# Issue times and landing delays by kind of transfer in a list scheduler's model of the DMA queue (attention, then two feed-forward layers, one core)

## The chip, the cores and the metric

The kernel runs on one core of a Trainium2 chip. The metric is the device time of one execution, in microseconds (us). The profile names the engines PE (TensorE matmul; PEld is its weight load), DVE (VectorE), ACT (ScalarE), POOL (GpSimd) and SP (SyncE, which here computes nothing and issues nearly all the DMA).

## The reference

```
attention, B=8, H=8, S=576, D=64:
  k_p, v_p = mean of k, v over groups of 8 positions       (72 keys each)
  attn_out = softmax(q k_p^T / 8) v_p
x  = attn_out as [4608, 512]
h  = x @ w_in [512, 2048];  g = max(h,0) + alpha*min(h,0);  x2 = g @ w_out [2048, 512]
logits = x2 @ w_gate [512, 8];  e(n) = argmax;  p(n) = softmax(logits)[e(n)]
out[n] = p(n) * ( max(x2[n] @ w1[e(n)], 0) @ w2[e(n)] )     w1 [8,512,1024], w2 [8,1024,512]
```

## The kernel before

All products are made of fp16 pairs: every operand is split into a high and a low half (a helper `s_hi` on ACT, DVE or POOL, then `s_lo` on DVE or POOL), and a product is three matmuls. Weights are converted on the core as well: `w_in` and `w_out` in the first 180 us, and the 16 expert matrices one after the other behind them, each loaded (`ew`, L1013), measured, split into two buffers `eo`, and stored to a scratch in DRAM (`wsc<-eo`, L1056).

The work comes in four strands that share the engines. (1) Attention, by tiles of 128 tokens (`plan_tile`, 36 of them): the load of q (`qr`, L528), its largest value `m` on DVE, the split, a DMA transpose `qT` (L543), the scores `sc` (L555, PE), eight exponentials `e` on ACT (L574), the weights `Abuf` in three pieces, a DMA transpose `AT` (L605), and the product with v, `xp` (L614, PE), which becomes `xT`. Keys and values come by batch (`plan_batch`): loads `raw` (L425), means, and a DMA transpose `KTb` (L466). (2) The first layer by blocks of 256 tokens (`plan_in`): products `hp` (L804), `r` on ACT (L818) and DVE (L822), `gT`; then `plan_out`: `yp` (L846). (3) The gate by blocks (`plan_gate`): `x2`, a DMA transpose `x2T` (L879), a store `x2d` (L882), logits `gp` (L910), a rank per expert, and two scatters to `table` from POOL (L985). (4) The expert layer by slots of 128 sorted tokens (`plan_slots`): a table read `srec` (L1244), a gather `x2g` from POOL (L1251), a DMA transpose `x2gT` (L1264), products `hp` (L1276) and `op` (L1294), a scatter of the result (L1304). Slots need the tokens of every earlier stage and all 16 converted matrices.

No order is written out by hand. Each step is handed to a class `Plan` with an engine (or a choice of engines), an estimated duration, the steps it depends on, the buffers it takes (`acq`) and gives back (`rel`), and a due time (`key`). `emit` runs a list schedule while the kernel is built: among all engines it takes the step that can start first by its model, at equal times the one with the lowest key, writes out its instructions, and moves the model's times on. The order in which each engine gets its instructions is thus fixed at build time. On the chip every engine works in that order and waits on semaphores; it doesn't pass a step that waits.

A step on SP is a DMA. The model has one clock `dma` for the queue. Before the change:

```python
            if o.eng == "SP":
                dma = max(dma, t + 1.1) + o.dur
                e["t"] = max(t + 0.5, dma - AHEAD)
                o.end = dma + 0.95
            else:
                e["t"] = o.end = t + o.dur
                o.end += o.lat + LAND.get(name, 0.0)
```

So with an idle queue a transfer that starts at t lands at t + 1.1 + `dur` + 0.95, and SP is free again 0.5 us after t. `dur` is 1.0 for `qT`, `x2T` and `x2gT`, 1.8 for `AT`, 1.2 for `KTb`; for loads it is bytes / 360e3 + 0.05, and 1.85 times that for q. A user on another engine is placed 0.2 us behind the landing. The expert loads have a fixed earliest time in the model's clock, 130 + 46 n us for n = 0 to 15. The last four slots are written out behind the plan, in branches.

Of the kernel before, what the change touches and what calls it, by code (L numbers as in the profile page):

```python
# [24 lines left out]

AHEAD = 3.0

LAND = {"ACT": 0.25, "DVE": 0.2, "POOL": 0.3}

PEN = {("DVE", "POOL"): (0.1, 0.0), ("DVE", "ACT"): (0.0, 0.0), ("ACT", "DVE", "POOL"): (0.0, 1.0, 1.0)}  # L30


class Op:
    __slots__ = ("eng", "dur", "fn", "deps", "key", "lat", "acq", "rel", "n", "users", "est", "end")

    def alts(self):
        return self.eng if isinstance(self.eng, tuple) else (self.eng,)
# [2 lines left out]
class Plan:  # L40
# [3 lines left out]
    def __init__(self, pools):  # L44
        self.ops, self.pools = [], pools

    def add(self, eng, dur, fn, deps=(), key=0.0, lat=0.0, acq=(), rel=(), order=()):
        o = Op()
        o.eng, o.dur, o.fn, o.key, o.lat, o.acq, o.rel = eng, dur, fn, key, lat, acq, rel
        o.deps = [d for d in deps if d is not None]  # L50
        order = [d for d in order if d is not None]
        o.n, o.users, o.est, o.end = len(o.deps) + len(order), [], 0.0, None
        for d in o.deps:
            d.users.append((o, True))
        for d in order:
            d.users.append((o, False))
        self.ops.append(o)
        return o

    def emit(self):  # L60
# [10 lines left out]
        dma = 0.0  # L71
        left = len(self.ops)
        log = []
        while left:
            best = None
            for name, e in engs.items():
                pick = None
                for k, i, o in e["ready"]:
                    t = max(e["t"], o.est)
                    for p, c in o.acq:  # L80
                        f = free[p]
                        t = max(t, sorted(f)[c - 1]) if len(f) >= c else None
# [28 lines left out]
            log.append((t, o))  # L111
            if o.eng == "SP":
                dma = max(dma, t + 1.1) + o.dur
                e["t"] = max(t + 0.5, dma - AHEAD)
                o.end = dma + 0.95
            else:
                e["t"] = o.end = t + o.dur
                o.end += o.lat + LAND.get(name, 0.0)
# [13 lines left out]
def attn_moe_moe_kernel(ctx: ExitStack, tc: tile.TileContext, q, k, v, w_in, w_out, alpha,  # L132
# [99 lines left out]
    SPQ = 10.0  # L232
# [32 lines left out]
    def dmat(nbytes):  # L265
        return nbytes / 360e3 + 0.05
# [51 lines left out]
    def first(key, shift):  # L318

        return key + shift if key < 70 else key  # L320
# [93 lines left out]
    def plan_batch(b, dl, users):  # L414
# [5 lines left out]
        for w in range(2):  # L420
            for c in range(nc_):
                def load(w=w, c=c):
                    sh = [SP_, hn, PL * D]
                    raws[w, c] = big(sh, F32, "raw0") if b == 0 else wk.tile(sh, F32, tag="raw", name="raw", bufs=2)
                    Y.dma_start(out=raws[w, c],  # L425
                                in_=(k, v)[w][b, hn * c:hn * c + hn].rearrange("h (s r) d -> s h (r d)", r=PL))

                def reduce(eng, w=w, c=c):
                    if c == 0:
                        kp[w] = wk.tile([SP_, H, D], F32, tag="kp", name="kp", bufs=2)  # L430
                    r, o_ = raws.pop((w, c)), kp[w][:, hn * c:hn * c + hn, :]
                    if eng == "DVE":
                        V.tensor_reduce(out=o_, in_=r.rearrange("p h (r d) -> p h d r", r=PL), axis=AX.X, op=ALU.add)
                        return
                    n = PL * D // 2
                    while n >= 2 * D:
                        G.tensor_tensor(out=r[:, :, 0:n], in0=r[:, :, 0:n], in1=r[:, :, n:2 * n], op=ALU.add)  # L437
                        n //= 2
                    G.tensor_tensor(out=o_, in0=r[:, :, 0:D], in1=r[:, :, D:2 * D], op=ALU.add)
                o = add("SP", dmat(72 * 2048 * hn), load, key=dl - 28 + (8 * w + c) * 8 / nc_, acq=[(pl, 1)])  # L440
                red.append(add(EITHER, (0.15 + hn * 0.87, pool(448 * hn) + 0.6), reduce, [o] + red[-1:],
                               key=dl - 26 + (8 * w + c) * 8 / nc_, rel=[(pl, 1)], acq=[("kp", 1)] if c == 0 else []))

# [48 lines left out]
                 rel=[("kp", 1)])  # L492
        o3 = add("DVE", 0.22, lambda: V.tensor_copy(kc[0:SP_, :, 3, :], kc[0:SP_, :, 0, :]), [o1], key=dl - 6)
        o4 = add("DVE", 0.22, lambda: V.tensor_copy(kc[0:SP_, :, 2, :], kc[0:SP_, :, 1, :]), [o2], key=dl - 5)
        oKT[b] = add("SP", 1.2, kT, [o2, o3, o4], key=dl - 4 - SPQ, acq=[("KT", 1)], rel=[("kc", 1)])
        o = osc[1]
        o1 = add(ANY, his(512), vhi, [o], key=dl - 4, acq=[("VS", 1)])
        o2 = add(EITHER, stt(512), vlo, [o1], key=dl - 4, acq=[("vlo", 1)], rel=[("kp", 1)])
        o3 = add("SP", 0.5, vdma, [o1], key=dl - 4)
# [19 lines left out]
    def plan_tile(i):  # L519
# [104 lines left out]
        def xlo():  # L624
            s_lo(xTt[j][:, 1, :, sl], xTt[j][:, 0, :, sl], c["xp"], S14)

        ends = [b for b in bs if LAST[b] == i]
        o = add("SP", dmat(262144) * 1.85, load, key=first(dl - 30, -6), acq=[("q", 1), ("att", 1)])
        o = add("DVE", dve(512), q1, [o], key=dl - 18)
        o = chain("DVE", pow2s(lambda: (c["m"], c["inv"], c["s"])), [o], dl - 18)  # L630
        o_s = o
        o = add(ANY, his(512), q2, [o], key=dl - 17, acq=[("qs2", 1)])
        o = add(EITHER, stt(512), lambda e: s_lo(c["qs"][:, :, 1, :], c["qs"][:, :, 0, :], c["q"], c["s"], e), [o], key=dl - 17,
                rel=[("q", 1)])
        o = add("SP", 1.0, q4, [o], key=dl - 16 - SPQ, acq=[("qT", 1)], rel=[("qs2", 1)])
# [10 lines left out]
        o = add(ANY, his(576), ahi, [o, o_c1], key=dl - 9, acq=[("A", 1)])  # L646
        o1 = add(EITHER, (dve(576), pool(576)), alo, [o], key=dl - 8, rel=[("e", 1)])
        o2 = add(("DVE", "ACT"), (0.22, 0.57), ahi2, [o], key=dl - 8)
        o = add("SP", 1.8, aT, [o1, o2], key=dl - 7 - SPA, acq=[("AT", 1)], rel=[("A", 1)])
        o = add("PE", pe(16, 128), av, [o] + [z for b in bs for z in oVS[b]], key=dl - 4, acq=[("gps", 1)],  # L650
                rel=[("AT", 1)] + [("VS", 1)] * len(ends))
        o = oXh[i] = add("ACT", act(512), xhi, [o, oXh.get(i - 1)], key=dl - 3, acq=[("xT", 1)] if half == 0 else [])
# [204 lines left out]
    def plan_gate(j):  # L857
# [5 lines left out]
        for t in range(2):  # L863
# [25 lines left out]
            o = add("SP", 1.0, y4, [o], key=k_ - SPY, acq=[("x2T", 1)])  # L889
            oT.append(o)  # L890
            oS.append(add("SP", dmat(262144), y5, [o], key=k_ + 1, rel=[("x2", 1)]))

        def ct_(t, p0, n, b):
            def f():
# [104 lines left out]
        oG2[j] = o  # L999
        oD = []  # L1000
        for t in range(2):
            oD.append(add("POOL", 1.1, lambda t=t: r3(t), [o, o4, o_tc] + oD, key=key + 6, lat=2.5,
                          rel=[("rec", 1)] if t else []))
        return oS, oD

# [1 line left out]
    def plan_expert(e, w, t0):  # L1007
# [50 lines left out]
        lds = [add("SP", dmat(1 << 20), lambda c=c: load(c), [oW["w_out"][-1]], key=t0 + c, acq=[("ew", 1), ("big", 1)]) for c in range(2)]  # L1058
        for x in lds:
            x.est = EXP0 + EXPD * (2 * e + w)  # L1060
        for c in range(4):
# [5 lines left out]
        for c in range(4):  # L1067
            ls = []
            for z in range(2):
                h = ph = add(ANY, his(512), lambda eng, c=c, z=z: hi(c, z, eng), [o, ph], key=t0 + 17 + 4 * c + 2 * z,  # L1070
                        acq=[("eo", 1)] if z == 0 else [])
                ls.append(add(EITHER, (1.0, 2.1), lambda eng, c=c, z=z: lo(c, z, eng), [h], key=t0 + 18 + 4 * c + 2 * z,
                              rel=[("ew", 1), ("big", 1)] if c % 2 and z else []))
            outs.append(add("SP", dmat(1 << 19), lambda c=c: store(c), ls, key=t0 + 20 + 4 * c, rel=[("eo", 1)]))
        return outs, o


# [134 lines left out]
    def plan_slots(c0, lo, n_slots, oD, o_x2, o_tab, o_exp, base, cond):  # L1212
# [3 lines left out]
        for i in range(n_slots):  # L1216
# [108 lines left out]
                continue  # L1325
            if n == cond + 1:
                tt = "big"
            o = add("SP", 0.1, tok, [o_r] + o_tab, key=key - 20, acq=[("srec", 1)])
            o = oGa[n] = add("POOL", 1.1, gather, [o] + o_x2, key=key - 18, lat=2.5, acq=[(tg, 1)])
            o_x = add("SP", 1.0, xT, [o], key=key - 15, acq=[(tt, 3 if tt == "big" else 1)], rel=[(tg, 1)])  # L1330
            oXt[n] = o_x

            if n >= cond:
# [113 lines left out]
```

## Time and profile before

| | us |
|---|---|
| median of 3 runs (lowest, highest) | 1445.33 (1442.6, 1445.35) |
| the profiled execution | 1447.14 |
| its span, first to last instruction | 1445.4 |
| PE busy | 1266.9 |
| DVE, POOL, ACT busy | 891.2, 778.7, 592.7 |

The profiled execution is 1.8 us above the median of the runs, and its span 1.7 us below its own time. A row of the timeline gives start, duration, engine, line, operation, the tile written and those read, a count, and in brackets the idle time before it and what ended that. Rows on SPq are DMA issues: their duration is the time that SP spent on the issue, not that of the transfer. The wait for a DMA is read off as the start of the user that was released by it.

### The profile page before, as it was taken

Reading aid. Unit: us, or ns where it says so; the run is one execution under the profiler, and the core shown is the slowest. Engines: PE = TensorE matmul, PEld = TensorE weight load, DVE = VectorE, ACT = ScalarE, POOL = GpSimd, SP = SyncE. Lnnn points to the kernel's source line nnn. Section 1 sums busy time; section 2 is a strip of 40 time slices with the busy share of each in tenths; the row PEclk is TensorE's granted clock in tenths of the full one; section 3 lists DMA queues with packets and bytes.
Section 4 is the critical chain, followed back from the end, with each engine's and each line's share of the span. In section 5 each row is a group of like instructions: output and inputs, shape, how many; then the busy total and the mean of one; then the engine's idle time right before and its main releaser. Section 6 shows DMA issues by size and latency. Waiting matters only on the chain. (4 is left out here: it accounts for less than half of the span.)

```text
span 1445.4 us, 30543 instructions
## 1 busy us (share of the span) xinstructions
PE 1266.9 (88%) x11555; PEld 875.0 (61%) x11555; DVE 891.2 (62%) x2051; ACT 592.7 (41%) x1324; POOL 778.7 (54%) x847
## 2 busy tenths in 40 slices
PE   0157799889898989999899999999799999999997
PEld 0145455646655755666576667765676776777674
DVE  7998788779667968868877777654252332332222
ACT  3786555536454645645564556541010110110010
POOL 6788967668677867647665666464122122112111
PEclk9998999999999999999999999999999999999999
DMA  9983397766777766676577476536658843593334
GB/s 241 290 196 91 98 222 149 191 152 163 190 149 171 201 190 130 176 195 153 126 189 199 122 149 146 172 103 197 168 133 240 198 91 74 167 304 104 74 96 166
DMA packets 314504, 237.21 MB, mean 164 GB/s; under 512 B 258351, under 2 KB 267695, under 8 KB 309488
## 3 DMA queue, kind: packets, MB, share of 16 engines
q1 hardware_dynamic: 306800, 214.98, 59.7%
q0 software_dynamic: 7552, 20.23, 4.7%
q8 instruction: 92, 1.51, 0.5%
q14 instruction: 60, 0.49, 0.1%
HBM read 263.52 MB, written 54.34 MB: 220 GB/s over the span
## 5 line engine op out<-in xcount | busy, mean ns | idle before, releaser
L804 PE MATMUL hp<-xT,w_in_hl 128*128 128x256 f16 x3456 | 409.8, 280 | 30.0 <-DVE r L822 22.4
L846 PE MATMUL yp<-w_out_hl,gT 128*128 128x512 f16 x1728 | 394.7, 386 | 9.6 <-POOL w_out_hl L201 5.4
L804 PEld LDWEIGHTS <-w_in_hl 128*128 128x128 f16 x3456 | 341.5, 100 | 83.1 <-DVE r L822 31.0
L846 PEld LDWEIGHTS <-gT 128*128 128x128 f16 x1728 | 168.2, 99 | 211.6 <-issue 22.6
L1276 PE MATMUL hp<-x2gT,ws 128*128 128x128 f16 x3744 | 217.9, 222 | 12.7 <-DMA x2gT<-x2g 8.1
L1276 PEld LDWEIGHTS <-ws 128*128 128x128 f16 x3744 | 215.7, 99 | 17.9 <-issue 12.0
L1294 PE MATMUL op<-ws,ht 128*128 128x512 f16 x936 | 205.7, 379 | 1.9 <-issue 1.9
L1282 ACT ACTIVATE hr<-hp 128x512 f32<-128x512 f32 x78 | 46.6, 597 | 374.1 <-PE hp L1276 369.9
L1294 PEld LDWEIGHTS <-ht 128*128 128x128 f16 x936 | 90.7, 98 | 107.6 <-issue 2.4
L574 ACT ACTIVATE e<-sc,nb,esc 128x72 f32<-128x72 f32 x288 | 116.3, 417 | 92.8 <-DVE inv L276 55.0
L1251 POOL DMA_INDIRECT x2g<-x2d,srec x41 | 43.5, 1061 | 202.3 <-DMA srec<-table 147.2
L822 DVE SCALAR_TENSOR_TENSOR r<-r,al,hp 128x256 f32<-128x256 f32 x288 | 124.0, 471 | 29.4 <-ACT r L818 29.1
L437 POOL TENSOR_TENSOR raw<-raw 72x256 f32<-72x256 f32 (+3 forms) x144 | 98.8, 686 | 65.2 <-DMA raw<-in_v_dram 30.4
L201 POOL TENSOR_TENSOR gT<-r,gT 128x512 f16<-128x512 f32 x99 | 124.8, 1260 | 8.3
L1286 DVE CAST ht<-hr 128x512 f16<-128x512 f32 x78 | 33.5, 430 | 151.5 <-ACT hr L1282 150.0
L183 ACT ACTIVATE gT<-r,cg 128x512 f16<-128x512 f32 x144 | 103.6, 724 | 55.9 <-DVE r L822 32.1
L183 ACT ACTIVATE eo<-ew,es 128x512 f16<-128x512 f32 x128 | 85.9, 713 | 97.7 <-DMA wsc<-eo 49.9
L1304 POOL DMA_INDIRECT out_dram<-so,srec x39 | 39.3, 1008 | 157.4 <-DVE cb L1299 60.4
L1301 DVE TENSOR_SCALAR so<-op,cb 128x512 f32<-128x512 f32 x39 | 29.3, 751 | 145.4 <-PE op L1294 145.3
L818 ACT ACTIVATE r<-hp 128x512 f32<-128x512 f32 x144 | 86.1, 598 | 75.0 <-POOL gT L201 49.4
L200 POOL TENSOR_SCALAR r<-r,cg 128x512 f32<-128x512 f32 x99 | 76.5, 772 | 60.9 <-ACT gT L183 59.9
L201 POOL TENSOR_TENSOR eo<-ew,eo 128x512 f16<-128x512 f32 x61 | 85.0, 1394 | 5.1
(221 smaller groups left out, 1524.9 us busy)
## 6 DMA issues: line engine op xcount, KB each, us to landing
ws<-wsc SPq DMA_DIRECT2D x166, 1024.0 KB
ew<-in_moe_w_dram SPq DMA_DIRECT2D x32, 1024.0 KB
wsc<-eo SPq DMA_DIRECT2D x64, 512.0 KB
x2d<-x SPq DMA_DIRECT2D x36, 256.0 KB
qr<-in_q_dram SPq DMA_DIRECT2D x32, 256.0 KB
w_in_f<-in_moe_w_in_dram SPq DMA_DIRECT2D x16, 512.0 KB
w_out_f<-in_moe_w_out_dram SPq DMA_DIRECT2D x16, 512.0 KB
raw<-in_k_dram SPq DMA_DIRECT2D x56, 144.0 KB
```

The costliest lines, as they stand in the source:

```text
L183: A.activation(out=hi, in_=src, func=ACTF.Copy, scale=s)
L200: G.tensor_scalar(out=src, in0=src, scalar1=s, scalar2=0.0, op0=ALU.mult, op1=ALU.add)
L201: G.tensor_tensor(out=lo, in0=src, in1=hi, op=ALU.subtract)
L437: G.tensor_tensor(out=r[:, :, 0:n], in0=r[:, :, 0:n], in1=r[:, :, n:2 * n], op=ALU.add)
L574: A.activation(out=c["e"][x], in_=c["scv"][x], func=ACTF.Exp, bias=c["nb"][:, z // 4, z % 4:z % 4 + 1], scale=c["esc"], accum_out=c["sm"][x])
L804: T.matmul(out=hp, lhsT=wt[:, a, kk, (m % 4) * 128:(m % 4 + 1) * 128], rhs=xTt[j][:, x, kk, :], start=(n == 0), stop=(n == 3 * KD - 1))
L818: A.activation(out=c["r"], in_=hps[j, m // 2], func=ACTF.Relu, scale=-1.0)
L822: V.scalar_tensor_tensor(out=c["r"][:, z], in0=c["r"][:, z], scalar=al1[:, m - 1 + z:m + z], in1=hps[j, m // 2][:, z], op0=ALU.mult, op1=A ...
L846: T.matmul(out=ypt[i], lhsT=gT[j][x][:, m, o_ * 128:(o_ + 1) * 128], rhs=W["w_out"][part][:, w, m % 4, :], start=(m == 0 and x == 0 and w ...
L1276: T.matmul(out=hp[:, f, :], lhsT=ws[kk // 2][:, kk % 2, a, ff * 128:(ff + 1) * 128], rhs=c["xT"][:, x * KD + kk, :], start=(z == 0), stop= ...
L1282: A.activation(out=c["hr", f4], in_=c["hp", f4], func=ACTF.Relu, scale=S24)
L1294: T.matmul(out=op, lhsT=c["ht"][:, x, f, :], rhs=ws[f // 4][:, f % 4, w, :], start=(f == 0 and x == 0 and w == 0), stop=(f == KF2 - 1 and ...
```

## The change

The model gets two tables by kind of transfer, and each DMA step a `kind`. SP is held for the time in `ISSUE` (0.45 us where a kind has none), and a transfer lands later by the time in `LATE`. The scatters to `table` and the gathers, issued on POOL, get a longer latency in the model (`lat` 2.5 to 4.0, and 2.5 to 3.3). No step, buffer, due time or duration is changed; what can differ in the program is the order in which steps are written out and the engine chosen for steps that have a choice.

```diff
+ISSUE = {"qT": 1.4, "AT": 1.9, "yT": 1.4, "kT": 1.5, "xT": 1.4, "v": 1.6, "tok": 0.8}
+LATE = {"kv": 1.5, "q": 1.0, "ew": 2.5, "st": 1.0, "qT": 1.0, "AT": 1.2, "yT": 1.0, "kT": 0.8, "v": 2.0, "x2": 2.0, "xT": 1.0}
...
                 dma = max(dma, t + 1.1) + o.dur
-                e["t"] = max(t + 0.5, dma - AHEAD)
-                o.end = dma + 0.95
+                e["t"] = max(t + ISSUE.get(o.kind, 0.45), dma - AHEAD)
+                o.end = dma + 0.95 + LATE.get(o.kind, 0.0)
...
-        o = add("SP", dmat(262144) * 1.85, load, key=first(dl - 30, -6), acq=[("q", 1), ("att", 1)])
+        o = add("SP", dmat(262144) * 1.85, load, kind="q", key=first(dl - 30, -6), acq=[("q", 1), ("att", 1)])
...
-        o = add("SP", 1.8, aT, [o1, o2], key=dl - 7 - SPA, acq=[("AT", 1)], rel=[("A", 1)])
+        o = add("SP", 1.8, aT, [o1, o2], kind="AT", key=dl - 7 - SPA, acq=[("AT", 1)], rel=[("A", 1)])
...
-            oD.append(add("POOL", 1.1, lambda t=t: r3(t), [o, o4, o_tc] + oD, key=key + 6, lat=2.5,
+            oD.append(add("POOL", 1.1, lambda t=t: r3(t), [o, o4, o_tc] + oD, key=key + 6, lat=4.0,
                           rel=[("rec", 1)] if t else []))
...
-            o = oGa[n] = add("POOL", 1.1, gather, [o] + o_x2, key=key - 18, lat=2.5, acq=[(tg, 1)])
-            o_x = add("SP", 1.0, xT, [o], key=key - 15, acq=[(tt, 3 if tt == "big" else 1)], rel=[(tg, 1)])
+            o = oGa[n] = add("POOL", 1.1, gather, [o] + o_x2, key=key - 18, lat=3.3, acq=[(tg, 1)])
+            o_x = add("SP", 1.0, xT, [o], kind="xT", key=key - 15, acq=[(tt, 3 if tt == "big" else 1)], rel=[(tg, 1)])
```

The other kinds are given in the same way: `kv` to the loads `raw`, `kT` to `KTb`, `v` to the two moves inside `VSb` (L477, L478), `qT`, `yT` to `x2T`, `x2` to the store `x2d`, `ew` to the expert loads, `st` to the expert stores, `tok` to the table read. The loads of `w_in` and `w_out` and of the slots' weights get none.

## Rows read from the trace of the kernel before

**Rows 1.** Busy time by stretch: from:to, length, engines, granted clock, DMA share, GB/s:
```profile
0.00:82.00 82.00, 8.40 (x103) 6.68 (x104) 69.14 (x115) 50.13 (x94) 59.23 (x70) 1.00 1.02 257
82.00:180.00 98.00, 70.64 (x524) 50.04 (x523) 79.82 (x134) 62.62 (x99) 87.06 (x81) 0.91 0.44 119
180.00:600.00 420.00, 379.00 (x3066) 251.70 (x3064) 328.50 (x790) 218.51 (x536) 303.66 (x364) 0.96 0.74 177
600.00:1000.00 400.00, 388.00 (x3150) 259.07 (x3151) 282.14 (x722) 214.11 (x516) 245.07 (x254) 0.98 0.61 155
...
1060.00:1419.74 359.74, 355.67 (x4001) 259.01 (x3999) 102.11 (x200) 39.41 (x66) 69.68 (x67) 1.00 0.58 156
```

**Rows 2.** Waits of PE from 180 to 1000 us: total, times, longest:
```profile
PE xp L614 <- DMA AT<-Abuf: 16.5, 9, 3.2
PE hp L804 <- DVE r L822: 15.3, 9, 5.3
PE gp L910 <- DMA x2T<-x: 10.1, 4, 3.2
```

**Rows 3.** Timeline of PE, stalls between 180 and 1000 us:
```profile
226.25 0.36 PE L910 MATMUL gp<-wg,x2T 128*128 128x16 f16 x8 [3.24 <-DMA x2T<-x]
...
278.58 5.41 PE L804 MATMUL hp<-xT,w_in_hl 128*128 128x256 f16 x48 [0.20 <-DVE r L822]
...
305.26 0.66 PE L614 MATMUL xp<-AT,VSb 128*64 128x128 f16 x16 [2.31 <-DMA AT<-Abuf]
...
376.91 7.08 PE L804 MATMUL hp<-xT,w_in_hl 128*128 128x256 f16 x48 [3.80 <-DVE r L822]
...
535.70 8.32 PE L804 MATMUL hp<-xT,w_in_hl 128*128 128x256 f16 x48 [5.31 <-DVE r L822]
...
601.73 0.66 PE L614 MATMUL xp<-AT,VSb 128*64 128x128 f16 x16 [1.85 <-DMA AT<-Abuf]
...
765.71 0.66 PE L614 MATMUL xp<-AT,VSb 128*64 128x128 f16 x16 [0.40 <-DMA AT<-Abuf]
...
862.80 0.70 PE L614 MATMUL xp<-AT,VSb 128*64 128x64 f16 x32 [0.34 <-DMA AT<-Abuf]
```

**Rows 4.** Timeline from 370 to 390 us, DVE and ACT ahead of a stall:
```profile
372.22 0.69 DVE L178 TENSOR_REDUCE m<-qr 128x1 f32<-128x512 f32 x1 [4.58 <-DMA qr<-in_q_dram]
...
373.20 0.41 ACT L574 ACTIVATE e<-sc,nb,esc 128x72 f32<-128x72 f32 x1 [10.66 <-DVE inv L272]
```

**Rows 5.** Busy time just behind a stall, columns as in rows 1:
```profile
535.70:544.00 8.30, 8.30 (x53) 6.35 (x54) 6.39 (x11) 5.98 (x13) 7.80 (x9) 0.64 1.07 330
```

**Rows 6.** Timeline of SP's DMA issues ahead of such stalls, from four stretches:
```profile
215.31 3.88 SPq L879 DMA_TRANSPOSE x2T<-x  x1
...
299.22 3.06 SPq L605 DMA_TRANSPOSE AT<-Abuf  x1
...
368.19 1.27 SPq L528 DMA_DIRECT2D qr<-in_q_dram  x1
...
596.88 1.82 SPq L605 DMA_TRANSPOSE AT<-Abuf  x1
```

**Rows 7.** Timeline of PE, the first product of the first layer:
```profile
83.90 5.82 PE L804 MATMUL hp<-xT,w_in_hl 128*128 128x256 f16 x35 [1.69 <-DVE xT L198]
...
106.37 1.07 PE L614 MATMUL xp<-AT,VSb 128*64 128x128 f16 x16 [6.73 <-DMA AT<-Abuf]
```

**Rows 8.** The line of `AT`, duration of the issue in ns, min/median/max:
```profile
L605 SPq DMA_TRANSPOSE AT<-Abuf x36: 1611/2746/5080, 62.0 to 942.6; - x36
```

**Rows 9.** The line of `x2T`, columns as in rows 8:
```profile
L879 SPq DMA_TRANSPOSE x2T<-x x36: 1237/1367/7391, 186.6 to 1029.0; - x36
```

**Rows 10.** The line of the table scatters, issue on POOL to landing:
```profile
DMA to landing us min/median/max: 3.7/5.0/11.3
```

**Rows 11.** Timeline of DVE ahead of the first product, pieces of the conversion:
```profile
73.42 1.20 DVE L178 TENSOR_REDUCE m<-w_in_t 128x1 f32<-128x1024 f32 x1
...
75.15 2.63 DVE L198 SCALAR_TENSOR_TENSOR w_in_hl<-w_in_t,sw,w_in_hl 128x1024 f16<-128x1024 f32 x1
```

More of the change, by code (lines that the diff above doesn't have):

```diff
@@ L33 @@
 class Op:
-    __slots__ = ("eng", "dur", "fn", "deps", "key", "lat", "acq", "rel", "n", "users", "est", "end")
+    __slots__ = ("eng", "dur", "fn", "deps", "key", "lat", "acq", "rel", "n", "users", "est", "end", "kind")
     def alts(self):
@@ L45, in __init__, with add @@
         self.ops, self.pools = [], pools
-    def add(self, eng, dur, fn, deps=(), key=0.0, lat=0.0, acq=(), rel=(), order=()):
+    def add(self, eng, dur, fn, deps=(), key=0.0, lat=0.0, acq=(), rel=(), order=(), kind=None):
         o = Op()
+        o.kind = kind
         o.eng, o.dur, o.fn, o.key, o.lat, o.acq, o.rel = eng, dur, fn, key, lat, acq, rel
@@ L439, in reduce @@
                     G.tensor_tensor(out=o_, in0=r[:, :, 0:D], in1=r[:, :, D:2 * D], op=ALU.add)
-                o = add("SP", dmat(72 * 2048 * hn), load, key=dl - 28 + (8 * w + c) * 8 / nc_, acq=[(pl, 1)])
+                o = add("SP", dmat(72 * 2048 * hn), load, kind="kv", key=dl - 28 + (8 * w + c) * 8 / nc_, acq=[(pl, 1)])
                 red.append(add(EITHER, (0.15 + hn * 0.87, pool(448 * hn) + 0.6), reduce, [o] + red[-1:],
@@ L494, in plan_batch @@
         o4 = add("DVE", 0.22, lambda: V.tensor_copy(kc[0:SP_, :, 2, :], kc[0:SP_, :, 1, :]), [o2], key=dl - 5)
-        oKT[b] = add("SP", 1.2, kT, [o2, o3, o4], key=dl - 4 - SPQ, acq=[("KT", 1)], rel=[("kc", 1)])
+        oKT[b] = add("SP", 1.2, kT, [o2, o3, o4], kind="kT", key=dl - 4 - SPQ, acq=[("KT", 1)], rel=[("kc", 1)])
         o = osc[1]
@@ L498, in plan_batch @@
         o2 = add(EITHER, stt(512), vlo, [o1], key=dl - 4, acq=[("vlo", 1)], rel=[("kp", 1)])
-        o3 = add("SP", 0.5, vdma, [o1], key=dl - 4)
+        o3 = add("SP", 0.5, vdma, [o1], kind="v", key=dl - 4)
         o4 = add("SP", 0.3, lambda: Y.dma_start(out=VS[b][2 * SP_ - 128:3 * SP_ - 128, 1], in_=st["vlo"]), [o2],
@@ L634, in plan_tile @@
                 rel=[("q", 1)])
-        o = add("SP", 1.0, q4, [o], key=dl - 16 - SPQ, acq=[("qT", 1)], rel=[("qs2", 1)])
+        o = add("SP", 1.0, q4, [o], kind="qT", key=dl - 16 - SPQ, acq=[("qT", 1)], rel=[("qs2", 1)])
         o_e = add("DVE", tiny(len(bs)), esc, [o_s] + [oSK[b] for b in bs], key=dl - 13)
@@ L888, in plan_gate @@
             o = add("DVE", dve(512), y3, [o], key=k_, rel=[("y", 1)])
-            o = add("SP", 1.0, y4, [o], key=k_ - SPY, acq=[("x2T", 1)])
+            o = add("SP", 1.0, y4, [o], kind="yT", key=k_ - SPY, acq=[("x2T", 1)])
             oT.append(o)
-            oS.append(add("SP", dmat(262144), y5, [o], key=k_ + 1, rel=[("x2", 1)]))
+            oS.append(add("SP", dmat(262144), y5, [o], kind="x2", key=k_ + 1, rel=[("x2", 1)]))
         def ct_(t, p0, n, b):
@@ L1056, in store @@
             Y.dma_start(out=wsc[r:r + 128, 2048 * c:2048 * (c + 1)], in_=cv[c].rearrange("p n c f -> p (n c f)"))
-        lds = [add("SP", dmat(1 << 20), lambda c=c: load(c), [oW["w_out"][-1]], key=t0 + c, acq=[("ew", 1), ("big", 1)]) for c in range(2)]
+        lds = [add("SP", dmat(1 << 20), lambda c=c: load(c), [oW["w_out"][-1]], kind="ew", key=t0 + c, acq=[("ew", 1), ("big", 1)]) for c in range(2)]
         for x in lds:
@@ L1073, in plan_expert @@
                               rel=[("ew", 1), ("big", 1)] if c % 2 and z else []))
-            outs.append(add("SP", dmat(1 << 19), lambda c=c: store(c), ls, key=t0 + 20 + 4 * c, rel=[("eo", 1)]))
+            outs.append(add("SP", dmat(1 << 19), lambda c=c: store(c), ls, kind="st", key=t0 + 20 + 4 * c, rel=[("eo", 1)]))
         return outs, o
@@ L1327, in plan_slots @@
                 tt = "big"
-            o = add("SP", 0.1, tok, [o_r] + o_tab, key=key - 20, acq=[("srec", 1)])
-            o = oGa[n] = add("POOL", 1.1, gather, [o] + o_x2, key=key - 18, lat=2.5, acq=[(tg, 1)])
-            o_x = add("SP", 1.0, xT, [o], key=key - 15, acq=[(tt, 3 if tt == "big" else 1)], rel=[(tg, 1)])
+            o = add("SP", 0.1, tok, [o_r] + o_tab, kind="tok", key=key - 20, acq=[("srec", 1)])
+            o = oGa[n] = add("POOL", 1.1, gather, [o] + o_x2, key=key - 18, lat=3.3, acq=[(tg, 1)])
+            o_x = add("SP", 1.0, xT, [o], kind="xT", key=key - 15, acq=[(tt, 3 if tt == "big" else 1)], rel=[(tg, 1)])
             oXt[n] = o_x
```

## The prediction, made before the result was known

> **What bounds the kernel now.** I read the busy time by stretch first, to see where PE, the busiest engine, is idle. The reader is to see five stages in [rows 1]. Up to 82 us PE is busy for 8.4 us: attention of the first tiles and the conversion of `w_in` come first, and DVE is full. From 82 to 180 us PE is idle for 27.4 us. From 180 to 1000 us it is busy for 767.0 of 820 us, so 53.0 us are lost in the steady state, 41.0 of them before 600 us. Behind 1060 us it is busy for 355.7 of 359.7 us; nothing is to be had there. The end therefore moves with the time at which the expert slots can start, and that with what PE loses before 1000 us.
>
> The waits of PE come next. Of the 53.0 us, 16.5 us in 9 waits are for `AT` and 10.1 us in 4 for `x2T`, both DMA transposes, and 15.3 us in 9 waits for DVE's `r` [rows 2]. Then the timeline around single stalls [rows 3]: two of the longest waits for `r`, 3.80 us at 376.91 and 5.31 us at 535.70, begin at a DMA as well. Ahead of the first, DVE stood for 4.58 us in front of `m<-qr`, for a load of q; ACT, waiting for DVE, stood for 10.66 us in front of the exponentials, with the first layer's `r` queued behind them; and PE ran out of free `hp` buffers [rows 4]. The second I put down to the same cause by its likeness. So 16.5 + 10.1 + 9.1 = 35.7 us of PE's loss have a late transfer at their root.
>
> A stall also costs clock. The same 48 matmuls take 5.41 us with the clock up and 7.08 and 8.32 us behind those two stalls [rows 3]; the mean granted clock of the 8.3 us behind the second is 0.64, a mixture of 2.4 and 1.2 GHz [rows 5]. The smaller difference, 1.67 us, is my price for one such drop.
>
> **What the change does, part by part.** It adds and removes no instruction; the planner's order is all that moves, with the choice of engine for the halves. So its price is that of the stalls that it removes and makes.
>
> *Landings.* By the old model `AT` is in the hands of its user 1.1 + 1.8 + 0.95 + 0.2 = 4.05 us after SP takes it up, by the new one 5.25. The trace shows 305.26 - 299.22 = 6.04 and 601.73 - 596.88 = 4.85 us [rows 3, 6]: the old figure is below both, the new one between them. `x2T` goes from 3.25 to 4.25, where a stalled one shows 226.25 - 215.31 = 10.94; q from 3.69 to 4.69, where the one above shows 372.22 - 368.19 = 4.03 [rows 4, 6]. So the direction is right. A step planned later lets the engine do something else first, and a stall shrinks by at most what the model adds. For `AT` that is 7 x 1.2 + 0.40 + 0.34 = 9.1 us (two of the nine stalls are shorter than 1.2), for `x2T` 4 x 1.0 = 4.0, for q 2 x 1.0 = 2.0: 15.1 us. In the first 180 us one wait for `AT` of 6.73 us [rows 7] gives another 1.2. Sum 16.3 us as the upper end, if at each of these places PE has other work that is ready.
>
> The lower end is nothing, if what is put first was also waiting. From 600 us on PE is 97% busy and work is at hand; before that it is 90% busy [rows 1]. Between the ends I take one half, 8 us, since 41 of the 53 us lie where work is scarcer.
>
> *Clock.* At most every stall that goes takes its drop along: 15 stalls x 1.67 = 25 us. A stall of 2.3 us that becomes 1.1 us may still cost the drop, so the lower end is nothing. I take 3 drops, 5 us: the shorter stalls are the ones that vanish whole.
>
> *Issue time.* The old model frees SP after 0.5 us, the new one after 1.9 us for `AT` and 1.4 us for `x2T`; measured medians are 2.75 and 1.37 us [rows 8, 9]. SP does the same work as before, so this costs nothing by itself; it moves loads that are planned behind a transpose to where the chip had them anyway. What hides an issue that is planned too late is the buffer it fills; if that is empty, DVE stands in front of `m<-qr` once more, 4.58 us at the one place shown [rows 4]. I count neither.
>
> *Scatters and gathers.* The scatter to `table` was modelled at 1.1 + 2.5 + 0.3 = 3.9 us and becomes 5.4; measured from issue to landing are 3.7 at least and 5.0 in the median [rows 10]. The second scatter of a pair waits for the first and POOL with it, with the split `gT` behind. The gain on PE lies between nothing and the rest of its waits for `r`, 15.3 - 9.1 = 6.2 us [rows 2, 3]; I take none.
>
> *Choice of engine.* A step that moves to another engine changes that engine's load. DVE is busy for 328.5 and POOL for 303.7 of 420 us from 180 to 600 [rows 1], so both have room; counted at nothing. Without that room a moved half would delay `gT` by its own length.
>
> Sum: 8 + 5 = 13 us off. The profiled execution of 1447.1 becomes 1434; its span of 1445.4 plus the 1.7 us around it, less 13. It is 1.8 us above the median of the runs, so the median goes from 1445.3 to about **1432.5 us**. Upper end of the gain 16.3 + 25 + 6 = 47, lower end 0.
>
> **One rule weighed.** The two `AT` rows say that 3.85 us from issue to landing, the old model's figure without its 0.2, is too short: 6.04 and 4.85 us [rows 3, 6]. The Trainium skill, "DMA: Bandwidth & Descriptors", section "Anatomy of one DMA", fits a DMA (there one issued from GpSimd) by 2.0 us + bytes / 436e3. `AT` has 128 x 16 x 128 x 2 = 524,288 bytes, which gives an estimate of 3.2 us; by it the old model was late enough, the added 1.2 us would buy nothing, and the sum would be 0 rather than 13. The trace disagrees with that figure for this transfer.
>
> **The rivals.**
>
> *The start becomes longer* (slower). The first product of a full block comes at 83.90 us and waits for `xT` [rows 7], which is the end of a chain with four transfers in it: the loads of q and k, `qT` beside `KTb`, and `AT`. All get 0.8 to 1.5 us more, the loads of `w_in` nothing. So at each the planner can put a piece of the conversion in front of attention's next step, on DVE, which is busy for 69 of 82 us [rows 1], and such a piece takes 1.20 to 2.63 us [rows 11]. Four pieces cost 4.8 to 10.5 us, and nothing hides them: PE has no other work yet. If the chip's transfers land before the piece is done, that is pure loss. With the upper end and a steady gain of only 4 us: 1445.3 + 10.5 - 4 = 1452. It decides from a first block that starts more than the steady state's gain later, 13 us in my sum, so behind about 97 us; with a steady gain of 4 behind 88 us. For it: DVE is the full engine there. Against it: due times put early attention first where both are ready.
>
> *The change doesn't do what it says* (no change). The stalls come not from the landing that the model had wrong but from transfers that meet others in the queue: 10.94 us for one `x2T` whose issue alone took 3.88 us, 4.85 against 6.04 for equal `AT`s [rows 6]. A constant of 1.0 can't foresee that; old stalls go and others come: 1445, within 3 us. By the Trainium skill's fit above it would be this case too.
>
> *Everything goes right* (faster by more): the stalls with a transfer at the root vanish with half of the drops: 16.3 + 13 = 29, 1416.
>
> **How the numbers follow.** Forecast 0.50, start longer 0.26, no change 0.14, everything right 0.10. 0.2% is 2.9 us, about what a measurement of this kernel can tell from no change. Faster takes the forecast and everything right: 0.60. No change: 0.14, of which 0.02 goes to slower, since reordering without a gain can as well lose 3 us: 0.12. Slower 0.28. The forecast's own range is 1422 (twice the drops, and three quarters of the stall time) to 1441 (a quarter of the sum). The range for all, with some 0.1 left out at either end: 1416, where everything goes right, to 1454, just above the longer start.
>
> **What would show it.** Right: waits of PE for `AT` and `x2T` from 180 to 1000 us fall from 26.6 to below 18 us; PE's busy time of that stretch rises in share; fewer stretches at the half clock; first block still between 80 and 90 us; expert slots begin some 13 us earlier, and the time from there to the end is the same. Wrong: the first block later than 90 us; equal waits of PE under other names, above all for DVE's `r`; expert conversions (whose earliest times are fixed in the planner's clock, which now runs slower against the work) crowding DVE and POOL before 600 us.

## The result, and the profile after

| | before | after |
|---|---|---|
| median of the runs (lowest, highest), us | 1443.96 (1437.24, 1445.35), 4 runs | 1393.83 (1389.46, 1400.39), 4 runs |
| the profiled execution, its span, us | 1447.14, 1445.4 | 1400.39, 1398.4 |
| mean granted clock of TensorE | 0.972 | 0.984 |

The ratio is 0.9666, 95% interval 0.9616 to 0.9715: 3.3% faster. Forecast were 1432.5 us, 0.9% below the 1445.3 us known then, in a range that ended at 1416. The four executions differ by 8 us before and by 11 us after, and the profiled one after is the slowest of its four; so the spans below differ by 47.0 us where the medians differ by 50.1. The four lines added at the top of the file shift the line numbers by 4 (`hp` is L808, `yp` L850, `AT` L609, `x2T` L883).

To see where the 47.0 us of the span went, both traces are cut at equal work and not at equal times: where block 1, 2, 14 and 17 of the first layer start their first product `hp`, and where slot 4 of the expert layer does. The counts of PE's matmuls in the cuts agree within 2. Busy time by stretch, before (columns as in [rows 1]):

```profile
0.00:118.80 118.80, 35.40 (x327) 28.28 (x327) 101.82 (x171) 79.01 (x138) 91.82 (x106) 0.97 0.95 242
118.80:208.90 90.10, 72.55 (x522) 42.68 (x520) 70.56 (x138) 47.04 (x88) 72.39 (x70) 0.94 0.43 115
208.90:826.00 617.10, 564.43 (x4566) 377.27 (x4563) 474.12 (x1147) 329.54 (x807) 432.62 (x495) 0.96 0.70 168
826.00:960.60 134.60, 134.26 (x1143) 91.81 (x1140) 93.06 (x235) 77.92 (x193) 80.29 (x79) 1.00 0.60 151
960.60:1055.20 94.60, 84.02 (x790) 61.39 (x789) 40.27 (x140) 16.84 (x28) 28.83 (x30) 0.95 0.56 154
1055.20:1445.40 390.20, 376.24 (x4227) 273.57 (x4224) 111.37 (x224) 42.39 (x71) 72.72 (x70) 0.99 0.57 152
```

And after:

```profile
0.00:122.00 122.00, 35.64 (x328) 28.50 (x329) 105.46 (x176) 82.64 (x141) 103.94 (x113) 0.97 0.92 236
122.00:198.90 76.90, 69.45 (x523) 41.83 (x521) 63.59 (x129) 40.70 (x83) 65.69 (x67) 0.98 0.48 125
198.90:780.80 581.90, 548.11 (x4564) 370.77 (x4560) 477.28 (x1154) 328.30 (x801) 438.09 (x495) 0.99 0.78 179
780.80:915.70 134.90, 134.30 (x1144) 91.89 (x1141) 95.29 (x238) 78.36 (x194) 74.45 (x76) 1.00 0.60 153
915.70:1013.00 97.30, 82.44 (x790) 59.78 (x789) 48.03 (x152) 16.93 (x29) 28.18 (x29) 0.93 0.62 157
1013.00:1398.40 385.40, 374.69 (x4227) 272.00 (x4224) 109.11 (x214) 42.42 (x71) 73.60 (x69) 0.99 0.54 153
```

Line by line the lengths differ by +3.2, -13.2, -35.2, +0.3, +2.7 and -4.8 us: 10.0 us are gained up to block 2, 35.2 us from block 2 to block 14, and 1.8 us in all behind that. Of the 35.2 us, 16.3 us are busy time (564.43 to 548.11 for the same matmuls, at a mean granted clock of 0.96 and 0.99), and 18.9 us are idle time (52.7 to 33.8). The reader is to see that nearly half of the gain of that stretch is not in any wait: it is the clock. The engines' loads hardly moved (DVE 474.1 to 477.3 us, POOL 432.6 to 438.1, ACT 329.5 to 328.3), so the choice of engine, counted at nothing, took little load off any of them.

The waits of PE from 180 to 940 us after, the answer to [rows 2]:

```profile
PE hp L808 <- DVE r L826: 17.5, 9, 5.6
PE xp L618 <- DMA AT<-Abuf: 6.0, 4, 2.7
PE gp L914 <- DMA x2T<-x: 4.1, 5, 1.9
```

Waits for the two transposes fell from 26.6 to 10.1 us; those for `r` did not fall (15.3 to 17.5).

The timeline of PE after, first with the answer to [rows 7], then two stalls of the steady stretch:

```profile
89.17 13.97 PE L808 MATMUL hp<-xT,w_in_hl 128*128 128x256 f16 x107 [1.19 <-DVE xT L202]
...
310.00 2.79 PE L808 MATMUL hp<-xT,w_in_hl 128*128 128x256 f16 x24 [2.50 <-DVE r L826]
...
458.10 4.46 PE L808 MATMUL hp<-xT,w_in_hl 128*128 128x256 f16 x24 [2.80 <-DVE r L826]
```

The first full block begins 5.3 us later than before (89.17 against 83.90), as the rival of the longer start had it: DVE begins with the conversion of `w_out` 4.4 us earlier, now ahead of that product (its first piece in the timeline of DVE, before and after).

```profile
83.83 1.44 DVE L721 SCALAR_TENSOR_TENSOR w_out_t<-wc,w_out_t 128x1024 int32<-128x1024 int32 x1
```
```profile
79.42 1.90 DVE L725 SCALAR_TENSOR_TENSOR w_out_t<-wc,w_out_t 128x1024 int32<-128x1024 int32 x1
```

And yet the start as a whole got shorter. It ends with the conversion of `w_out`, on which the first `yp` waits. POOL's last piece of it, before and after (timeline of POOL):

```profile
176.35 2.50 POOL L201 TENSOR_TENSOR w_out_hl<-w_out_t,w_out_hl 128x1024 f16<-128x1024 f32 x1
```
```profile
161.69 2.55 POOL L205 TENSOR_TENSOR w_out_hl<-w_out_t,w_out_hl 128x1024 f16<-128x1024 f32 x1
```

PE's waits for these pieces between block 1 and block 2, before and after:

```profile
PE yp L846 <- POOL w_out_hl L201: 5.4, 3, 4.1
PE yp L846 <- DVE w_out_hl L198: 2.4, 1, 2.4
```
```profile
PE yp L850 <- POOL w_out_hl L205: 1.8, 2, 1.4
```

Of the 13.2 us gained there, 6.0 us are these waits, 4.1 us other idle time, above all PE's waits for `r` (5.7 to 1.0), and 3.1 us busy time at a higher clock (0.94 to 0.98).

### The profile page after: what moved, and what is told of

The parts are those of the page before. It is cut to its first block, busy times and chain, and to the rows that moved or that the text cites. A ratio compares the mean times of both kernels' runs of the same rounds, so it can differ in the third digit from the quotient of the medians.

```text
span 1398.4 us, 30543 instructions
## 1 busy us (share of the span) xinstructions
PE 1244.6 (89%) x11555; PEld 864.8 (62%) x11555; DVE 898.7 (64%) x2060; ACT 589.4 (42%) x1316; POOL 783.9 (56%) x845
## 5 line engine op out<-in xcount | busy, mean ns | idle before, releaser
L808 PE MATMUL hp<-xT,w_in_hl 128*128 128x256 f16 x3456 | 400.7, 277 | 28.9 <-DVE r L826 20.3
L850 PE MATMUL yp<-w_out_hl,gT 128*128 128x512 f16 x1728 | 385.4, 380 | 2.4 <-POOL w_out_hl L205 1.8
L808 PEld LDWEIGHTS <-w_in_hl 128*128 128x128 f16 x3456 | 337.5, 99 | 76.8 <-DVE r L826 21.7
L850 PEld LDWEIGHTS <-gT 128*128 128x128 f16 x1728 | 165.9, 98 | 201.3 <-issue 10.0
L1280 PE MATMUL hp<-x2gT,ws 128*128 128x128 f16 x3744 | 215.3, 220 | 13.2 <-DMA x2gT<-x2g 11.9
L1280 PEld LDWEIGHTS <-ws 128*128 128x128 f16 x3744 | 212.8, 98 | 18.8 <-issue 14.0
L205 POOL TENSOR_TENSOR gT<-r,gT 128x512 f16<-128x512 f32 x106 | 129.7, 1224 | 8.8
L441 POOL TENSOR_TENSOR raw<-raw 72x256 f32<-72x256 f32 (+3 forms) x138 | 105.6, 766 | 27.9 <-DMA raw<-in_v_dram 12.1
L204 POOL TENSOR_SCALAR r<-r,cg 128x512 f32<-128x512 f32 x106 | 83.2, 785 | 60.1 <-ACT gT L187 55.8
L205 POOL TENSOR_TENSOR eo<-ew,eo 128x512 f16<-128x512 f32 x63 | 79.3, 1259 | 5.3
```

What stands on the lines that cost most here:

```text
L204: G.tensor_scalar(out=src, in0=src, scalar1=s, scalar2=0.0, op0=ALU.mult, op1=ALU.add)
L205: G.tensor_tensor(out=lo, in0=src, in1=hi, op=ALU.subtract)
L808: T.matmul(out=hp, lhsT=wt[:, a, kk, (m % 4) * 128:(m % 4 + 1) * 128], rhs=xTt[j][:, x, kk, :], start=(n == 0), stop=(n == 3 * KD - 1))
L850: T.matmul(out=ypt[i], lhsT=gT[j][x][:, m, o_ * 128:(o_ + 1) * 128], rhs=W["w_out"][part][:, w, m % 4, :], start=(m == 0 and x == 0 and w ...
L1280: T.matmul(out=hp[:, f, :], lhsT=ws[kk // 2][:, kk % 2, a, ff * 128:(ff + 1) * 128], rhs=c["xT"][:, x * KD + kk, :], start=(z == 0), stop= ...
```

## The experiments

Each was compared with the kernel before on the same chip, whose medians there were 1437.3 to 1440.7 us; "ratio" is to that kernel, with its 95% interval. The edits are shown in short form, against the changed kernel where nothing else is said. Theories: **A**, the landing delays of the transposes, before which PE stood; **B**, those of loads and stores, before and behind which DVE, ACT and POOL stood; **C**, the issue times; **D**, luck, any reshuffled order being better than the one before.

### One part alone, and a reshuffle

Issue times alone (`e1_issue_only`):

```diff
-LATE = {"kv": 1.5, ...}
+LATE = {}
...
-lat=4.0 / lat=3.3
+lat=2.5 / lat=2.5
```

> Only the issue times by kind; landing delays and the POOL latencies as before. Theory A (the landing delays did it: the engines no longer stand in order behind a transfer that the model lands too early): within 10 us of before, 1434 to 1454, PE's waits for AT and x2T about as before (22 us in the steady blocks). Theory C (the issue times did it: SP's queue is planned where the chip has it): most of the gain, 1395 to 1410. Theory D (luck: the order before was a poor one and any reshuffle does better): faster by 20 us or more as well.

Measured 1441.2, ratio 1.0032 (1.0008 to 1.0056): within 0.3% of before. C alone is out, and so is D in its simple form, that any reshuffle does better.

Landing delays alone (`e2_late_only`):

```diff
-ISSUE = {"qT": 1.4, ...}
+ISSUE = {}          # and ISSUE.get(o.kind, 0.5)
...
-lat=4.0 / lat=3.3
+lat=2.5 / lat=2.5
```

> Only the landing delays by kind; SP's issue time is 0.5 us for all and the POOL latencies are as before. A: nearly the whole gain, 1390 to 1405, with few stretches at the half clock. C: within 10 us of before. D: anywhere between 1395 and 1445, without relation to PE's waits for DMA.

Measured 1423.6, ratio 0.9916 (0.9890 to 0.9942): a quarter of the gain. A had said 1390 to 1405 and C within 10 us of before; both miss. The longest of its waits of PE from block 2 to block 14 grew, against 10.1 us in 4 before:

```profile
PE gp L914 <- DMA x2T<-x: 20.0, 7, 4.9
```

POOL's latencies alone (`e3_lat_only`: `ISSUE = {}` with 0.5 for all, `LATE = {}`, `lat` 4.0 and 3.3):

> Only the latencies of the table scatters and the gathers, both issued on POOL; SP's model as before. A and C: within 10 us of before, 1434 to 1454. D: faster by 20 us or more, as any reshuffle.

Measured 1439.1, ratio 1.0019 (0.9999 to 1.0038): no gain, as A and C had it.

A reshuffle without a better model (`e6_nudge_up`, the kernel before with one constant nudged):

```diff
-                o.end = dma + 0.95
+                o.end = dma + 1.0
```

> The kernel before with one constant nudged, the landing of every SP transfer 1.0 instead of 0.95 us after the queue's clock: the order is reshuffled, and the model is no better. A and C: 1434 to 1454, the scatter of orders being below 10 us. D: the order before was an unlucky one, so this one comes out 20 us or more faster.

Measured 1441.0, ratio 1.0021 (0.9996 to 1.0045). Every engine's order is another one, some 100 steps change between DVE and POOL, about as many as in the change, and the time is the same within 0.3%. Four orders made without longer landing delays on SP (before, and these three without `LATE`) lie between 1.000 and 1.003: the gain is neither luck of reshuffling nor a matter of steps that move to another engine.

### Which landing delays, and with what

Landing delays and issue times, POOL's latencies as before (`e11_late_issue`: the change with `lat=2.5` in both places):

> Landing delays and issue times by kind, the POOL latencies as before. Alone, the landing delays gave 0.8% and the issue times nothing; together with the POOL latencies 3.3%. Theory E (landing and issue need each other: with landings right, PE still stood 25.9 us in front of x2T, whose issue comes late because SP is modelled as free after 0.5 us): most of the gain, 1385 to 1400, PE's waits for x2T below 10 us. Theory F (landing and POOL latencies need each other): about as the landing delays alone, 1415 to 1425. Theory D (luck of one order): no relation, 1390 to 1430.

Measured 1403.1, ratio 0.9748 (0.9695 to 0.9801). With the issue times, worth nothing alone, this is 1.7% faster than the landing delays without them. E still misses its range (1385 to 1400) by 3 us, and PE's waits for `x2T` fell from 20.0 to 14.0 us, not below 10. The 1.7% compare one order with one other.

Landing delays of the five transposes alone, and of loads and stores alone (`e4_late_transposes`, `e5_late_rest`; `ISSUE` and `lat` as before):

```diff
+LATE = {"qT": 1.0, "AT": 1.2, "yT": 1.0, "kT": 0.8, "xT": 1.0}                       # e4
+LATE = {"kv": 1.5, "q": 1.0, "ew": 2.5, "st": 1.0, "v": 2.0, "x2": 2.0}              # e5
```

> Of the landing delays only those of the five DMA transposes; nothing else. Theory A (it is PE in front of its transposes): as all landing delays together, 1418 to 1428. Theory B (it is DVE, ACT and POOL in front of loads and behind stores): as before, 1432 to 1445.

> Of the landing delays only those of the loads and stores (kv, q, ew, st, v, x2); nothing else. B: as all landing delays together, 1418 to 1428, with DVE's and ACT's waits for DMA down. A: as before, 1432 to 1445.

Measured 1415.1, ratio 0.9814 (0.9784 to 0.9844), and 1423.0, ratio 0.9885 (0.9852 to 0.9919). Each alone does as well as both together without issue times (0.9916) or better. Neither A nor B is out, and the parts don't add.

The waits tell the two apart where the times don't. PE's waits from 180 to 1000 us, to be held against [rows 2], with e4 first and then e5:

```profile
PE gp L914 <- DMA x2T<-x: 6.5, 4, 2.8
PE xp L618 <- DMA AT<-Abuf: 5.7, 3, 3.1
```
```profile
PE xp L618 <- DMA AT<-Abuf: 24.0, 9, 8.8
PE hp L808 <- DVE r L826: 1.4, 3, 0.9
```

And DVE's waits for the loads of q in the same stretch, before, in e4 and in e5:

```profile
DVE m L178 <- DMA qr<-in_q_dram: 42.1, 12, 6.9
```
```profile
DVE m L182 <- DMA qr<-in_q_dram: 35.3, 15, 4.3
```
```profile
DVE m L182 <- DMA qr<-in_q_dram: 18.2, 6, 4.9
```

The four orders with the old landings show what reshuffling alone does: `AT` 11.1 to 21.5 us, `x2T` 9.0 to 18.1, `r` 11.6 to 23.5, q 29.0 to 42.1. Delays of the transposes took the waits for the two transposes below that, and those for `r` to 7.8 us; delays of loads and stores took the waits for q and for `r` below it, and those for `AT` above it. So what the model lands later is waited for less in these two orders, and the fall of `r` to 1.4 us speaks for late loads at its root, as the prediction read it. It is no rule for every order: with both groups delayed (e2) PE stood before `x2T` for 20.0 us.

Landing delays and issue times of the transposes (`e13_transposes_both`; `lat` as in the change):

```diff
-ISSUE = {"qT": 1.4, "AT": 1.9, "yT": 1.4, "kT": 1.5, "xT": 1.4, "v": 1.6, "tok": 0.8}
+ISSUE = {"qT": 1.4, "AT": 1.9, "yT": 1.4, "kT": 1.5, "xT": 1.4}
-LATE = {"kv": 1.5, "q": 1.0, "ew": 2.5, ...}
+LATE = {"qT": 1.0, "AT": 1.2, "yT": 1.0, "kT": 0.8, "xT": 1.0}
```

> Landing delays and issue times for the five DMA transposes alone, POOL's latencies as in the change; loads, stores and the moves of v as before. Theory A with E (PE in front of transposes that the model issues and lands too early): nearly the whole gain, 1390 to 1405, waits of PE for x2T and AT below 12 us from block 2 to block 14. Theory B has a share of its own: 1405 to 1420, with waits of DVE for q and of POOL for the raw loads as long as before.

Measured 1413.2, ratio 0.9809 (0.9765 to 0.9854). A with E misses its range by 8 us, and B's (1405 to 1420) holds; DVE's waits for q, 33.2 us from block 2 to block 14 against 41.1, stayed long, as B had it. The issue times and POOL's latencies added nothing to e4 (0.9814). The waits of PE from block 2 to block 14 for `AT`, before, and for both transposes in e13:

```profile
PE xp L614 <- DMA AT<-Abuf: 16.1, 8, 3.2
```

```profile
PE xp L618 <- DMA AT<-Abuf: 18.4, 7, 4.4
...
PE gp L914 <- DMA x2T<-x: 1.3, 2, 0.8
```

`AT` was modelled as in the change, and PE stood before it for 18.4 us, no less than before the change (16.1). With the same figures for `AT` it was 1.6 us in e11 and 5.4 us in the change. So a transfer's own delay in the model doesn't by itself set the wait for that transfer.

The changed kernel nudged in the same way (`e8_after_nudge`, 0.95 to 1.0 in the change):

> The changed kernel with the same nudge as the kernel before got, 1.0 instead of 0.95: another order by a model that is as good. If the gain is the model's, within 10 us of the changed kernel, 1383 to 1403. If the changed kernel has a lucky order (D), it falls back by 15 us or more, to 1405 to 1435.

Measured 1393.8, ratio 0.9682 (0.9652 to 0.9712): another order, the same gain, as the model's theory had it.

### Where: the start and the rest

The new model for steps placed before 150 us of the planner's clock only, and behind it only (`e14_start_only`, with `lat=2.5`; `e15_steady_only`):

```diff
-                e["t"] = max(t + ISSUE.get(o.kind, 0.45), dma - AHEAD)
-                o.end = dma + 0.95 + LATE.get(o.kind, 0.0)
+                e["t"] = max(t + (ISSUE.get(o.kind, 0.45) if t < 150.0 else 0.5), dma - AHEAD)    # e15: t >= 150.0
+                o.end = dma + 0.95 + (LATE.get(o.kind, 0.0) if t < 150.0 else 0.0)                # e15: t >= 150.0
```

> Landing delays and issue times by kind only for steps that the model places before 150 us; behind that, and for POOL's latencies, the old model. Theory G (two separate gains: about 10 us at the start, where the conversion of w_out ends earlier, and some 35 us between 200 and 800 us): block 2 of the first layer starts at about 199 us instead of 209, and the median is 8 to 14 us below before, 1424 to 1432. If the start's lead is lost again later, or is no effect of the model: within 5 us of before.

> The complement of the start alone: the old model for steps placed before 150 us, the changed model behind that, POOL's latencies as in the change. If the two gains add up (theory G; the start alone gave 1.5%): block 2 of the first layer at about 209 us as before, 1410 to 1422. If the start's new order is what the later blocks need: as before, 1432 to 1445. If the steady stretch carries it all: 1393 to 1405.

Measured 1417.8, ratio 0.9854 (0.9809 to 0.9899), and 1416.7, ratio 0.9841 (0.9789 to 0.9892). The two gains add up to 3.0% of the change's 3.3%, but not as G had it: e15 lies in its range, e14 6 us below its own, since it gained more than the start's 10 us. Its row from block 2 (at 198.5 us, 10.4 us earlier than before) to block 14, and that of e15 (block 2 at 207.1):

```profile
198.50:792.40 593.90, 551.31 (x4563) 372.04 (x4560) 464.49 (x1157) 328.31 (x803) 426.54 (x494) 0.98 0.73 175
```
```profile
207.10:798.40 591.30, 549.27 (x4563) 371.82 (x4560) 475.85 (x1155) 325.14 (x798) 433.87 (x503) 0.99 0.79 176
```

e14's later stretch is 23.2 us shorter than before (617.1) under the old model. Its order there is another one, since the planner's state at 150 us is; what in it is better, these runs don't tell.

### How late

One landing delay and one issue time for all transfers of SP (`e9_uniform`; `lat` as in the change), and the same with twice the delay (`e19_uniform_double`):

```diff
-                e["t"] = max(t + ISSUE.get(o.kind, 0.45), dma - AHEAD)
-                o.end = dma + 0.95 + LATE.get(o.kind, 0.0)
+                e["t"] = max(t + 0.9, dma - AHEAD)
+                o.end = dma + 0.95 + 1.3                                                          # e19: 2.6
```

> One landing delay (1.3 us) and one issue time (0.9 us) for every transfer of SP, POOL's latencies as in the change: the model is as late on average, and knows no kinds. If it is the lateness that matters: 1385 to 1405. If it is the kinds: 1410 to 1435.

> One landing delay of 2.6 us and one issue time of 0.9 us for every transfer of SP. One delay of 1.3 us gave 2.2% against 3.3% by kinds. If lateness is what counts and not kinds: near the doubled delays by kind, 1372 to 1390. If kinds count: 1390 to 1410.

Measured 1405.2, ratio 0.9777 (0.9711 to 0.9843), and 1392.2, ratio 0.9666 (0.9612 to 0.9719). By the ranges set beforehand e9 lies at the very end of lateness's (1405), and e19 2 us inside the range of the kinds (1390 to 1410). But without any kinds they have two thirds of the change's gain and all of it: kinds are not needed for a gain of that size, and lateness counts. That kinds add something on top stays open.

The delays of the change times 2, 3 and 5 (`e10_double`, `e16_triple`, `e17_quintuple`: each number of `LATE` multiplied, the rest as in the change):

> Landing delays doubled, the rest as in the change. If the model of the change is still too early for what the chip does (x2T and q show 7 us and more where PE or DVE stands before them), a further gain, 1370 to 1390. If the figures of the change are about right, buffers are held too long in the model and PE finds less work: 1395 to 1420.

> Landing delays three times those of the change. Theory H (the gain comes from a model that is as late as the chip; AT would now be planned 7.65 us behind its issue where stalled ones show 6.4 in the median): worse than the doubled delays, 1380 to 1400. Theory I (the gain is slack: the later the model lands a transfer, the less an engine stands in order before it, and no buffer is short): equal to or better than the doubled ones, 1365 to 1380.

> Five times, 6 us for AT and 12.5 us for the expert loads on top of the queue's clock. H: much worse, 1400 to 1430, since buffers are held in the model for longer than on the chip and attention and expert weights are planned too late. I: within 10 us of the doubled ones.

Measured: 1377.3, ratio 0.9572 (0.9531 to 0.9613); 1430.0, ratio 0.9927 (0.9899 to 0.9955); 1491.8, ratio 1.0380 (1.0322 to 1.0438). The doubled delays gain further, within their range. At three and five times H has the direction (worse), but both are slower than its ranges, by 30 and 62 us. Slack without end (I) is out; the best lateness lies below three times that of the change. The doubled kernel from block 2 to block 14, its row and its two largest groups of waits of PE:

```profile
199.40:755.70 556.30, 541.67 (x4564) 369.14 (x4561) 464.09 (x1150) 323.77 (x796) 439.38 (x503) 1.00 0.80 186
```
```profile
PE mp L312 <- DVE xT L202: 4.0, 2, 2.6
PE hp L808 <- DVE r L826: 2.7, 3, 1.2
```

The mean granted clock is 1.00, and the same 4564 matmuls keep PE busy for 541.67 us. At five times the delays PE's largest waits there are for ACT, in front of the scores of attention:

```profile
PE sc L559 <- ACT e L578: 29.5, 7, 8.3
PE hp L808 <- ACT xT L187: 7.2, 2, 3.7
```

The doubled delays nudged (`e18_double_nudge`, 0.95 to 1.0), and delays set by kind to what traces show where an engine stood before the transfer (`e20_fitted`; the new figures):

```diff
+ISSUE = {"qT": 1.45, "AT": 2.75, "yT": 1.4, "kT": 1.5, "xT": 1.4, "v": 1.75, "tok": 0.8}
+LATE = {"kv": 1.7, "q": 2.5, "ew": 2.5, "st": 0.3, "qT": 2.4, "AT": 2.4, "yT": 3.0, "kT": 2.0, "v": 2.5, "x2": 1.0, "xT": 2.0}
```

> The doubled delays with the nudge of 0.95 to 1.0: whether their gain over the change belongs to the model or to one order. Model: 1367 to 1387, as the doubled delays. One lucky order: 1385 to 1400.

> Delays and issue times per kind set to what the traces show where an engine stood in front of the transfer (AT issue 2.75; landing delays kv 1.7, q 2.5, ew 2.5, st 0.3, qT 2.4, AT 2.4, yT 3.0, kT 2.0, v 2.5, x2 1.0, xT 2.0), POOL's latencies as in the change. Theory H (as late as the chip): as good as the doubled delays or better, 1365 to 1382. If the doubled delays are good for another reason: 1385 to 1405.

Measured 1395.5, ratio 0.9692 (0.9653 to 0.9731), and 1412.2, ratio 0.9813 (0.9780 to 0.9846). The first lies in the range of the lucky order: a nudge costs the doubled delays 1.2 of their 4.3%, and they are then no better than the change. Whether once or twice the delays are better these orders don't tell. The second is 30 us above H's range and 7 us above the other one: "the closer to the chip kind by kind, the better" gets no support. Two orders of one late model differed by 1.2% here and by 0.2% in the change, and many of these kernels lie no further apart: kinds against one delay (e9, e19), POOL's latencies (e11 against the change, 0.8%), and the issue times (1.7% from e2 to e11, nothing from e4 to e13) can't be ranked by one order each.

### The plan and the chip

The planner's own clock can be read beside the trace: the end that `emit` gives to the last part of the last `yp`, and the end of its last matmul in the trace. The left column isn't a time of the chip; it is what the order was made for.

```
kernel            last yp in the plan   on the chip   the chip behind its plan
before                    894              1003               109
e2_late_only              893               978                85
the change                891               958                67
e10_double                898               933                35
e18_double_nudge          898               953                54
e20_fitted                904               974                70
e16_triple                926               987                62
e17_quintuple            1008              1043                35
```

(us; the last column is from unrounded times, one profiled execution of each.) The change didn't make the plan shorter: it was within 1% of 895 us in every kernel up to twice the delays. It made the chip keep to it, 42 of the 47 us. The three other orders with the old landings (e1, e3, e6) end 101 to 106 us behind their plans; all with later landings, up to twice, 35 to 90 us. At three and five times the delays the plan itself grows, by 31 and 114 us over that of the kernel before, and that is what the overshoot costs.

## Why the prediction was wrong

**What bounds the kernel: right.** The end moved with the start of the expert slots: slot 4 began 42.2 us earlier (1055.2 to 1013.0), and from there to the end 4.8 us more were gained where nothing had been expected.

**Mechanism: right in its kind, wrong in its detail.** Orders planned with later landings hold fewer stalls, and a model that is too late loses again: shown by the row of delays from none to fivefold. But "a stall shrinks by at most what the model adds", the ground of the first term, is the step that failed. It gave an upper end of 15.1 us for the steady stretch, and 8 us were taken for all landings; idle time between blocks 2 and 14 fell by 18.9 us, the waits for `AT` by 10.5 us where 9.1 were allowed and those for `x2T` by 6.0 where 4.0 were, and in e13 the waits for `AT` didn't shrink at all with its own delay in the model. A planner's estimate that moves reorders every engine (e6, where 0.05 us did), and a stall then goes whole or another comes.

**Clock: the term that was mis-sized.** Three drops of 1.67 us, 5 us, were taken out of 15. Busy time for equal work fell by 16.3 us between blocks 2 and 14 and by 22.3 us over the span (1266.9 to 1244.6). The size was to be read in [rows 1] without counting drops: 379.0 us at a mean clock of 0.96 and 388.0 us at 0.98 are, as an estimate, 15 + 8 = 23 us lost to the clock. The upper end of the working, 25 us, was close to that, and was discounted.

**The start: a gain that the sum left out.** The working allowed it 1.2 us at most, and the rival a loss. The rival's first half happened: conversion moved ahead of the first product, and the first full block came 5.3 us later. Its second half, "pure loss", didn't: the stage ends with the conversion of `w_out`, whose last piece on POOL began 14.7 us earlier, and block 2 began 10.0 us earlier, as it did in e14 with the new model at the start alone (10.4). The step that failed was to price the delay at the first product and not at the wait that ends the stage; PE's 7.8 us of waits for `w_out_hl` between 118.8 and 208.9 us were in the trace. That the earlier conversion accounts for all of the 10.0 us isn't shown: 6.0 us of it are these waits.

**Issue times: right alone, open in company.** Counted at nothing; alone they gave nothing (1.0032). Beside all landing delays one order with them was 1.7% faster (e11), beside those of the transposes none (e13, with POOL's latencies). Costing the parts one by one couldn't show such a thing.

**Waits for `r`: left out with luck.** The working put 9.1 of the 15.3 us down to late loads of q, and e5 speaks for that reading (1.4 us left). In the change they stayed, at 17.5 us, although DVE's waits for q fell from 42.1 to 16.1; in the doubled delays they were 2.7 us. What holds them in the change isn't shown.

**POOL's latencies: right** to be left out, as far as they were run alone (1.0019).

**The rule weighed.** By the Trainium skill's fit ("DMA: Bandwidth & Descriptors", section "Anatomy of one DMA") the added delays would buy nothing. The runs with landing delays gained 0.8 to 4.3% up to twice the change's; the two rows that disagreed with the fit were the better guide.

**The range.** Of the 47.0 us, 18.9 are idle time and 16.3 clock between blocks 2 and 14, where 8 and 5 were taken; 10.0 come from the start, where at most 1.2 had been allowed, and 1.8 from behind block 14. The range stopped at a gain of 29, since the ends of the two terms were not allowed to meet, though the stalls that go can be those that cost the clock. That the working's upper end was also 47 us is chance: 10 of the measured ones come from where it allowed 1.2.

What stays open: why e14 gains in a stretch that its model leaves as it was; whether kinds do better than one delay; and which steps of the order, in the change, spare PE the stalls. That the cushion behind each transfer keeps one late landing from being handed on through engines that work in order is argued from [rows 4], the waits in e4 and e5, and the table of plan and chip, not shown step by step.

## What to carry to other kernels

When an order is fixed ahead from a model, compare the trace with the plan itself, say at the end of each strand: a plan that the chip couldn't keep was the loss here, and later landings by 0.8 to 2.5 us per transfer, with the rest of the change, were worth 3.3%. Price a stall of PE with its clock behind it, from the mean granted clock of the whole stretch, and a delay at the wait that ends its stage. Before one order's gain is read as a parameter's merit, nudge a constant: here two orders of nearly the same model differed by 0.2% twice and by 1.2% once, and the best single kernel (0.9572) was partly such luck.

## What the hardware showed that was not expected

The same stretch of 4564 matmuls took 564.4, 548.1 and 541.7 us of busy time at mean granted clocks of 0.96, 0.99 and 1.00, in three orders of one program. Single stalls showed it too: 24 matmuls took 2.79 us behind a stall of 2.50 us, at a granted clock of 1.00, and 4.46 us behind one of 2.80 us, at a mean of 0.62, a mixture of 2.4 and 1.2 GHz. And an issue of the same DMA transpose `AT` held SP for 1.7 to 8.4 us after the change, 2.8 in the median:

```profile
L609 SPq DMA_TRANSPOSE AT<-Abuf x36: 1685/2844/8394, 62.6 to 901.6; - x36
```
